# Transposing y on the sync queue instead of on TensorE: the background phases of a long convolution with a phase MLP

## The chip, the cores and the metric

The kernel runs on one core of a Trainium2 chip. That core has five engines that run side by side: TensorE (PE; its weight loads are listed as PEld), VectorE (DVE), ScalarE (ACT), GpSimd (POOL) and SyncE (SP). Transfers between HBM and the on-chip memory are issued by an engine's queue (here SP, ACT and POOL) and carried out by 16 DMA engines. The metric is the device time of one execution in microseconds, less is better. Before the change it is 1988.78 us, the median of three runs (1986.59 to 1993.94).

## The reference

```python
def _attn_ref(x, h):                       # x: 8 x 5696 x 128, h: 5696 x 128
    L = 2 * S
    Yf = np.fft.rfft(x, n=L, axis=1) * np.fft.rfft(h, n=L, axis=0)[None]
    return np.fft.irfft(Yf, n=L, axis=1)[:, :S, :]

def _moe_ref(x, w_theta, w_tok_r, w_tok_i, w_ch):
    theta = x @ w_theta
    zr, zi = x * np.cos(theta), x * np.sin(theta)
    y = einsum('ts,bsd->btd', w_tok_r, zr) + einsum('ts,bsd->btd', w_tok_i, zi)
    u = x + y
    return u + np.maximum(u @ w_ch, 0.0)
```

The output of the first function is the input of the second. Call it y, as the kernel does: 5696 tokens, 8 batches, 128 channels. The token mixing, two 5696 x 5696 matrices against 8 x 128 columns, is by far the largest part of the arithmetic.

## The kernel before

First comes the convolution, with matmuls in place of the FFTs. It leaves y in HBM as `yt_hbm`, channel by channel: for each of 128 channels and each batch a row of 5696 tokens. The token mixing follows. It runs in two passes p over the input tokens (0 to 2815, then 2816 to 5631; the last 64 tokens apart). In each pass the output tokens are taken in pairs of row blocks of 128: block tt together with block 22 + tt. A pair goes over 11 blocks of input tokens in four stretches of 3, 3, 3 and 2. Each pair forms seven products by Strassen's scheme instead of eight, in the order M3, M4, M5, M2, M1, M7, M6, and adds them into four tiles c at the pair's end (VectorE, L1399). The weights arrive through POOL's queue in a ring of six places (L669), are transposed by VectorE (`wt`, L972), summed for Strassen's products (L981), and used by TensorE (L1392).

The input of the second pass is not ready when the first pass begins. Its zr and zi are made in the background of the first pass, in "background phases": one for each of the 23 token tiles 22 to 44 and each half of the batches, 46 in all, one in every stretch of a pair but the last, so three per pair. A list `spread` holds them, each as functions:

- `load` (L995): the sync queue loads `yT`, 128 channels x 4 batches x 128 tokens. It is called two phases ahead; the pool has three buffers.
- `first` (L1000 to L1003), behind the second product of the stretch: TensorE transposes `yT` into PSUM (`tpz`, tag "misc", four transposes), ScalarE copies it to the small room (`yt_room`, 512 columns at the end of the ring's tile, one room for all), and the sync queue stores it as token rows in `y2_hbm`. The pairs later add these rows as the `x` of `x + y` (`addend`, L1085).
- `second`, behind the fifth product: `phases_b`. TensorE makes theta from `yT` (L552, PSUM tag "misc"). ScalarE rounds and copies (L554, L555), VectorE subtracts (L556), ScalarE takes the absolute value and the two sines (L572, L573, L576). VectorE multiplies both with the rows in the small room (L587, L588). The sync queue stores the results as four pieces in `z_hbm` (L611).

Tile 44 has 64 tokens only. The function `aside` takes the next entry from `spread`, runs its `first`, calls the `load` of the entry after the next, and later runs its `second`. After the phases, `spread` goes on with `bg_left` entries, and in the second pass with `u_stage` entries, which also use the small room.

What the sync queue does in a pair beside that: four loads of addends (L1085), four stores of partial sums (L1107). A queue works in its order, so an issue that waits holds up all that stands behind it. In the first pass from the third pair on, the order on each engine is the tile scheduler's; it sorts by readiness and priority, and puts in the waits between writers and readers of a tile. Each transfer of the sync queue also takes one of eight semaphores in turn.

Of the kernel before, what the change touches and what calls it, by code (L numbers as in the profile page):

```python
# [23 lines left out]
def kernel(  # L24
# [10 lines left out]
    nc = tc.nc  # L35
    B, S, D = x.shape
    assert D == 128
    P = 128
# [14 lines left out]
    y2_hbm = y2_hbm_h.ap()  # L53
# [43 lines left out]
    yt_hbm = nc.dram_tensor("yt_hbm", (D, B, S), BF16, kind="Internal").ap()  # L97
# [554 lines left out]
    def small(at, n):  # L652
        return ring["all"][:, WB + BT + at:WB + BT + at + n]
# [5 lines left out]
    def yt_room():  # L659
        return small(0, 4 * P).rearrange("p (b n) -> p b n", b=4)  # L660
# [79 lines left out]
    def load_b(p, j, pool, eng=nc.scalar):  # L740
        t_ = tile_b(p, j, pool)
        for z in range(2):
            if p == 0:
                eng.dma_start(
                    t_[:, :4096].rearrange("p (q r w) -> p q r w", q=2, r=2)[:, :, z],
                    zr_hbm[j].rearrange("q i (s r) z n -> (i s) q r (z n)", r=2)[:, :, z])
            else:
                eng.dma_start(
                    t_[:, z * 2048:(z + 1) * 2048].rearrange("p (q n) -> p q n", q=2),
                    z_hbm[z, j].rearrange("q i (s r) n -> (i s) q (r n)", r=2))  # L750
# [98 lines left out]
    for g, (bp, dh) in enumerate(groups):  # L849
        st = {}  # L850
# [85 lines left out]
    spread = []  # L936

    def open_mixing():

        nonlocal bp, cp, wlp, ybp  # L940
        xa.close()
        bp, cp, wlp, ybp = (ctx.enter_context(tc.tile_pool(name=name, bufs=bufs, reuse_waits="tile"))
                            for name, bufs in (("bpool", 1), ("cpool", 1), ("wlpool", 2), ("ybpool", 3)))
        load_b(0, NJ - 2, bp)
        sides["cs"] = [addend(0, n, t, h) for n, (t, h) in enumerate(((0, 1), (22, 0), (0, 0), (22, 1)))]
        load_b(0, NJ - 1, bp)
        spread.extend(bg_phase(t, h) for t in list(range(24, 34)) + [22, 23, 44] + list(range(34, 44)) for h in range(2))
        spread.extend(bg_left(g) for g in range(0, NT, 4))
        spread[0][0]()
        spread[1][0]()  # L950

    for j in range(NJ):
        owed += [(j, k, lambda j=j, k=k: sum_ops(bts_of[0][j])[k]()) for k in range(5)]
# [12 lines left out]
    def half(z, ti, h):  # L966

        return z[ti].rearrange("p b d -> p (b d)")[:, h * 512:h * 512 + 512]
# [20 lines left out]
    def bg_phase(t, h):  # L989
        st = {}  # L990
        m = min(P, S - t * P)

        def load():
            st["yT"] = yT = ybp.tile([P, 4, P], BF16, tag="yb", name="yT")
            nc.sync.dma_start(yT[:, :, :m], yt_hbm[:, 4 * h:4 * h + 4, t * P:t * P + m])  # L995

        def first():
            tpz = mps.tile([P, 4, P], BF16, tag="misc", name="tpz")
            for b in range(4):
                nc.tensor.transpose(tpz[:m, b, :], st["yT"][:, b, :m], ident_bf)  # L1000
            st["yb"] = yb = yt_room()
            nc.scalar.activation(yb[:m], tpz[:m], AF.Copy)  # L1002
            nc.sync.dma_start(half(y2_hbm, t, h)[:m], yb[:m].rearrange("p b d -> p (b d)"))  # L1003

        def second():
            phases_b(t, st["yb"], 4 * h, 4, st["yT"][:, :, :m], cp, mps, "misc", nc.vector,
                     tags=where_bg["tags"], m=m)
        return load, first, second

    def bg_left(g):  # L1010

        n = min(4, NT - g)
        st = {}

        def load():
            st["wl"] = wl = ybp.tile([P, 4, 2, KL], BF16, tag="yb", name="wl")
            for r, a in enumerate((moe_w_tok_r, moe_w_tok_i)):
                if g + n < NT:
                    nc.gpsimd.dma_start(
                        wl[:, :n, r, :],  # L1020
                        bass.AP(tensor=a.tensor, offset=a.offset + g * P * S + 2 * H,
                                ap=[[S, P], [P * S, n], [1, KL]]))
                else:
                    assert n == 1
                    nc.gpsimd.dma_start(
                        wl[:S_last, 0, r, :],
                        bass.AP(tensor=a.tensor, offset=a.offset + g * P * S + 2 * H,
                                ap=[[S, S_last], [1, KL]]))

        def first():  # L1030
            wl = st["wl"]
            m = P if g + n < NT else S_last
            tpw = mps.tile([P, 4, P], BF16, tag="misc", name="tpw")
            for t in range(n):
                nc.tensor.transpose(tpw[:, t, :m],
                                    wl[:m, t, :, :].rearrange("p r k -> p (r k)"),
                                    ident_bf[:m, :m])
            wls = yt_room()
            nc.scalar.activation(wls[:, :n, :m], tpw[:, :n, :m], AF.Copy)
            nc.sync.dma_start(wl_hbm[:, g:g + n, :m], wls[:, :n, :m])  # L1040
        return load, first, nothing
# [30 lines left out]
    def addend(p, k, ti, h, m=P):  # L1072

        tag = f"c{k}"
        if p == 1:
            tag = ("c0", "c1", "c2", "c3", "red", "mag")[tags["n"] % 6]
            tags["n"] += 1
        c = cp.tile([P, 512], F32, tag=tag, name=f"c{k}")
        if p == 0 and ti in (22, 23):
            yT = cp.tile([P, 4, P], BF16, tag=f"yy{k}", name=f"yy{k}")  # L1080
            nc.sync.dma_start(yT, yt_hbm[:, 4 * h:4 * h + 4, ti * P:ti * P + P])
            return c, yT
        if p == 0:
            yy = cp.tile([P, 512], BF16, tag=f"yy{k}", name=f"yy{k}")
            nc.sync.dma_start(yy[:m], half(y2_hbm, ti, h)[:m])  # L1085
            return c, yy
        nc.sync.dma_start(c[:m], half(cp_hbm, ti, h)[:m])
        return c, c
# [104 lines left out]
    nxt, second, st, ms_of = None, None, {}, {}  # L1193
    ordered = ExitStack()
    for i, (k, p, tt, j0, s0, nj) in enumerate(stretches):
# [40 lines left out]
                in_place(j)  # L1236
        if woven:
            nxt, step = nxt
        def aside(first_of, second_of):
            nonlocal second  # L1240
            if first_of and spread and (p == 1 or (tt > 1 and not end_of_pair)):
                where_bg["tags"] = ("c2", "c3") if j0 + s0 == TJ else ("red", "mag")
                _, first, second = spread.pop(0)
                first()
                if len(spread) > 1:
                    spread[1][0]()
            if second_of and second is not None:
                second()
                second = None

        if tt is None:
            if p:
                aside(True, False)
# [6 lines left out]
            for j in range(nj):  # L1260
                jj = j0 + s0 + j
                for r in range(2):
                    b = [x[:, r, :] for x in bts[jj]]
# [6 lines left out]
            if p:  # L1270
                aside(False, True)
                for f in {0: (lambda: safe(NJ - 2),), TJ: (lambda: safe(NJ - 1),),
                          2 * TJ: (lambda: in_place(NJ - 2), lambda: in_place(NJ - 1))}.get(j0 + s0, ()):
                    f()
# [64 lines left out]
        if classic:  # L1339
            for n in range(4):  # L1340
                for j in range(nj):
                    last = product(a, j0 + s0 + j, j, n, range(2))
                    if p == 0 and (n * nj + j) % 4 != 3:
                        sum_some(1)
                    if p == 0 and (n * nj + j) % 3:
                        y_some(1, last)
                if end_of_pair and n % 2:
                    (c12, z12), (c21, z21), (c11, z11), (c22, z22) = cs
                    out_of = (((c11, z11, 0), (c12, z12, 1)), ((c21, z21, 2), (c22, z22, 3)))[n // 2]
                    for h, (c, z, m_) in enumerate(out_of):  # L1350
                        if p:
                            nc.tensor.matmul(ms[m_], wl[n // 2], zl[h], start=False, stop=True)
                            nc.vector.tensor_tensor(c, z, ms[m_], op=add)
                            continue
                        if n == 1:
                            nc.tensor.matmul(ms[m_], ident_bf, z, start=False, stop=True)
                        else:
                            for b in range(4):
                                nc.tensor.matmul(ms[m_][:, b * D:(b + 1) * D], z[:, b, :], ident_bf,
                                                 start=False, stop=(b == 3))  # L1360
                        nc.scalar.activation(c, ms[m_], AF.Copy)
                aside(n == 0, n == 2)
# [92 lines left out]
```

## Time and profile before

| | |
|---|---|
| median of three runs | 1988.78 us (1986.59 to 1993.94) |
| profiled execution | 1985.37 us, span 1983.6 us, mean granted TensorE clock 0.993 |
| TensorE busy | 1922.2 us (97%) |
| VectorE busy | 1560.4 us (79%) |
| ScalarE busy | 642.7 us (32%) |
| DMA engines, mean busy share 560 to 960 us | 0.92 |
| tpz transposes (L1000) | 184, first at 464.7, last at 988.7 us |
| copies to the small room (L1002) | 46, median 597 ns |
| y stores from the small room (L1003) | issue median 535 ns, landing 1.7/4.5/6.9 us (min/median/max) |
| yT loads (L995) | landing 2.3/5.0/10.1 us |

The profile is of one execution. A group's line names the line of the kernel, the engine, the operation, what it writes and reads, how often, and then busy time and mean; idle time before an instruction stands in brackets with what ended it. On a timeline the two leading numbers are start and duration in us, several equal instructions in a row being merged. Matmuls are pipelined: their listed durations overlap, and the distance between starts is what one costs. The "share" of the DMA engines is the time that packets took, summed over queues, against the 16 engines' time; it can exceed 1.

### The profile page before, as it was taken

The numbers are of one execution on the slowest core, as the hardware profiler recorded it, in microseconds if no ns is written. First come the engines' busy times: TensorE is split into PE (matmuls) and PEld (weight loads), VectorE is DVE, ScalarE is ACT, GpSimd is POOL, SyncE is SP. The second block draws the span as 40 slices with busy tenths as digits, with TensorE's granted clock in tenths as the row PEclk, the third lists the DMA queues.
The fourth block names the chain that finished last, engine by engine and source line by source line (L and its number), as shares of the span: only waits on it lengthen the run. The fifth ranks groups of instructions, "written<-read, shape, count | busy, mean of one in ns | idle before, by whom it ended". The sixth has DMA issues, their size and how long they took to land.

```text
span 1983.6 us, 41205 instructions
## 1 busy us (share of the span) xinstructions
PE 1922.2 (97%) x15757; PEld 1060.6 (53%) x15757; DVE 1560.4 (79%) x2855; ACT 642.7 (32%) x960; POOL 976.7 (49%) x1746
## 2 busy tenths in 40 slices
PE   5899999899999999999999999999999999999998
PEld 5798997544444444444444444444444444444444
DVE  8877888876888888888877678686776877767767
ACT  6899997812233333323310001011111111111111
POOL 8636324445354544536475645445455354453540
PEclk9899999999999999999999999999999999999999
DMA  9999869998898998989999899768789688787883
GB/s 114 71 102 141 96 108 256 260 234 159 178 176 176 172 175 160 185 171 177 173 166 162 143 298 194 122 122 155 137 140 155 125 151 145 130 152 130 150 151 83
DMA packets 487829, 312.01 MB, mean 157 GB/s; under 512 B 184071, under 2 KB 448423, under 8 KB 486647
## 3 DMA queue, kind: packets, MB, share of 16 engines
q0 software_dynamic: 322160, 156.41, 62.3%
q1 hardware_dynamic: 158304, 139.22, 23.9%
q10 hardware_dynamic: 7168, 13.76, 2.0%
q8 instruction: 123, 2.02, 0.4%
q14 instruction: 74, 0.61, 0.1%
HBM read 354.37 MB, written 90.29 MB: 224 GB/s over the span
## 4 chain that ended last, share of the span: by engine, by line
PE 69%; DMA 4%; DVE 3%; POOL 1%; issue 1%; ACT 0%; ACTq 0%; DVEq 0%; SPq 0%; POOLq 0%
PE m L1392 61%; PE m L1304 3%; DMA b<-z_hbm 2%; DVE c L1399 1%; POOL ring L669 1%; PE utp L1052 1%; PE v L1059 1%; PE m L1396 1%; DVE wt L972 1%; PE m L1268 1%; DMA ring<-in_moe_w_tok_r_dram 1%; PE tpz L1000 0%; PE misc L1304 0%; PE theta_ps L552 0%; DMA ring<-in_moe_w_tok_i_dram 0%
## 5 line engine op out<-in xcount | busy, mean ns | idle before, releaser
L669 POOL DMA_DIRECT2D ring<-in_moe_w_tok_i_dram x720 | 388.0, 547 | 658.3 <-DVE wt L972 576.0
L669 POOL DMA_DIRECT2D ring<-in_moe_w_tok_r_dram x720 | 387.1, 548 | 117.8 <-DVE wt L972 68.5
L972 DVE STREAM_TRANSPOSE wt<-ring 128x384 f32<-128x384 f32 (+2 forms) x720 | 359.7, 525 | 99.9 <-PE m L1392 65.6
L1392 PE MATMUL m<-b,wt 128*128 128x512 bf16 x1640 | 388.3, 379 | 1.9 <-DVE wt L972 1.7
L1392 PEld LDWEIGHTS <-wt 128*128 128x128 bf16 x1804 | 176.1, 98 | 215.8 <-DVE wt L972 4.3
L1399 DVE TENSOR_TENSOR c<-c,m 128x512 f32<-128x512 f32 x412 | 266.7, 672 | 0.4 <-PE m L1392 0.4
L1054 ACT ACTIVATE ring<-utp 128x512 bf16<-128x512 bf16 x85 | 50.7, 597 | 575.8 <-PE utp L1052 575.8
L139 POOL DMA_DIRECT2D x<-in_x_dram x128 | 99.6, 807 | 89.8 <-PE ps L255 83.5
L432 PE MATMUL ps<-r_u,uv 128*128 128x128 f16 x1024 | 126.2, 223 | 6.6 <-DVE uv L408 3.0
L432 PEld LDWEIGHTS <-uv 128*128 128x128 f16 x2048 | 121.7, 100 | 8.8 <-issue 4.6
L432 PE MATMUL ps<-r_v,uv 128*128 128x128 f16 x1024 | 125.8, 223 | 0.0
L408 DVE TENSOR_TENSOR uv<-xs,hs 128x1024 f16<-128x1024 f16 x192 | 117.4, 662 | 5.1 <-ACT xs L404 3.6
L1304 PE MATMUL m<-b,wt 128*128 128x512 bf16 x440 | 106.8, 380 | 3.9 <-DMA b<-zr_hbm 2.3
L1049 ACT ACTIVATE ub<-c 128x512 bf16<-128x512 f32 x88 | 55.1, 628 | 161.4 <-DVE c L1399 81.9
L404 ACT ACTIVATE xs<-ps 128x1024 f16<-128x1024 f32 x96 | 88.4, 992 | 5.6 <-PE ps L278 3.1
L1304 PEld LDWEIGHTS <-wt 128*128 128x128 bf16 x528 | 50.9, 98 | 62.6 <-issue 5.0
L554 ACT ACTIVATE red<-theta_ps,magic 128x512 f32<-128x512 f32 (+1 forms) x46 | 31.6, 687 | 128.8 <-PE theta_ps L552 99.5
L1002 ACT ACTIVATE ring<-tpz 128x512 bf16<-128x512 bf16 (+1 forms) x46 | 27.4, 597 | 140.6 <-PE tpz L1000 124.0
L880 DVE TENSOR_TENSOR b<-b 128x1024 bf16<-128x1024 bf16 x100 | 61.6, 685 | 4.6 <-DMA y_hbm<-b 4.4
L278 PEld LDWEIGHTS <-w_t 64*128 64x128 f16 x3240 | 55.0, 98 | 14.2 <-issue 8.0
L1061 DVE SCALAR_TENSOR_TENSOR c<-v,c 128x512 f32<-128x512 f32 x88 | 60.1, 685 | 2.6 <-PE v L1059 2.6
L572 ACT ACTIVATE mag<-red 128x512 f32<-128x512 f32 (+1 forms) x46 | 29.0, 631 | 93.5 <-DVE red L556 93.5
(2935 smaller groups left out, 3679.9 us busy)
## 6 DMA issues: line engine op xcount, KB each, us to landing
ring<-in_moe_w_tok_r_dram POOLq DMA_DIRECT2D x352, 96.0 KB, 4.6
ring<-in_moe_w_tok_i_dram POOLq DMA_DIRECT2D x352, 96.0 KB, 4.9
ring<-in_moe_w_tok_r_dram POOLq DMA_DIRECT2D x352, 80.0 KB, 4.5
ring<-in_moe_w_tok_i_dram POOLq DMA_DIRECT2D x352, 80.0 KB, 3.9
cp_hbm<-c SPq DMA_DIRECT2D x88, 256.0 KB, 2.4
c<-cp_hbm SPq DMA_DIRECT2D x88, 256.0 KB, 4.6
out_dram<-c SPq DMA_DIRECT2D x88, 256.0 KB, 4.4
yy<-y_hbm SPq DMA_DIRECT2D x84, 128.0 KB, 2.4
```

Of the source, the lines that this page charges most:

```text
L139: nc.gpsimd.dma_start(x16[p0:p1, e, n0:n0 + 16, :HD], bass.AP(tensor=src.tensor, offset=src.offset + (p0 * N2 + n0) * D + dh * HD, ap=[[N2 ...
L404: nc.scalar.activation(xs[:, :, :, :CHK[c][1]], ps, AF.Copy)
L408: nc.vector.tensor_tensor(uv[e][:, :, :, c0:c0 + ck], xs_of[c][:, e:e + 1, :, :ck].to_broadcast([P, 2, HD, ck]), h_part(c), op=mult)
L432: nc.tensor.matmul(o, uv_t[e][:, r, d * K1:d * K1 + P], r_, start=(r == 0), stop=(r == 1))
L669: nc.gpsimd.dma_start(wb[32 * i:32 * i + 32, :ng, :nj * 64], bass.AP(tensor=a.tensor, offset=a.offset + row0 * S + p * H + i * QR + j0 * 6 ...
L880: return [lambda f=f, x=x: f(*x) for f, x in ((nc.vector.tensor_sub, (bt[M3], b12, b22)), (nc.vector.tensor_sub, (bt[M4], b21, b11)), (nc. ...
L972: nc.vector.transpose(wt.rearrange("p j t r -> p (j t r)").bitcast(F32).rearrange("p (j g t) -> p g j t", j=TJ, g=4)[:, :ng, :nj], wb[:, : ...
L1049: nc.scalar.activation(ub[:m].rearrange("p b d -> p (b d)"), c[:m], AF.Copy)
L1061: nc.vector.scalar_tensor_tensor(c[:m], v[:m], 0.0, c[:m], op0=ALU.max, op1=ALU.add)
L1304: ins = nc.tensor.matmul(ms[n // 2 * 2 + h], a[n][:, j, :, r], bts_of[p][jj][n % 2 * 2 + h][:, r, :], start=(n % 2 == 0 and jj == 0 and r ...
L1392: nc.tensor.matmul(ms[q], a[q][:, j, :, r], bts[jj][q][:, r, :], start=(jj == 0 and r == 0), stop=(jj == NJ - 1 and r == 1 and q not in left))
L1399: nc.vector.tensor_tensor(c, z, ms[q], op=op)
```

## The change

For full tiles the rows in the small room no longer come from TensorE and ScalarE. A new function `turned` takes the small room and issues four transposing transfers on the sync queue, one per batch, each of 128 channels x 128 tokens straight out of `yt_hbm`. `first` of a full tile only issues the store of the rows. `turned` is called for the next phase right after the `second` of the one before, and for the first phase when the mixing opens. `yT` is still loaded, for theta. The half tile 44, `bg_left` and `u_stage` stay as they were.

```diff
         spread[0][0]()
         spread[1][0]()
+        spread[0][3]()
...
+        def turned():
+            if m == P:
+                st["yb"] = yb = yt_room()
+                for b in range(4):
+                    nc.sync.dma_start_transpose(yb[:, b:b + 1, :], yt_hbm[:, 4 * h + b, t * P:t * P + P])
+
         def first():
+            if m == P:
+                nc.sync.dma_start(half(y2_hbm, t, h), st["yb"].rearrange("p b d -> p (b d)"))
+                return
             tpz = mps.tile([P, 4, P], BF16, tag="misc", name="tpz")
             for b in range(4):
                 nc.tensor.transpose(tpz[:m, b, :], st["yT"][:, b, :m], ident_bf)
...
-        return load, first, second
+        return load, first, second, turned
...
+        def turn_next():
+            if spread and len(spread[0]) == 4:
+                spread[0][3]()
+
         def aside(first_of, second_of):
...
-                _, first, second = spread.pop(0)
+                _, first, second = spread.pop(0)[:3]
                 first()
                 if len(spread) > 1:
                     spread[1][0]()
             if second_of and second is not None:
                 second()
                 second = None
+                turn_next()
```

## The prediction

> **What bounds the kernel now.** I read the page first (engine shares, then the costliest groups), then the stretches of the stage in which the background phases run (465 to 1000 us), then that stage's timeline.
>
> The page's first two lines, and from the view of line 1002 the copy that goes:
>
> ```profile
> span 1983.6 us, 41205 instructions
> PE 1922.2 (97%) x15757; PEld 1060.6 (53%) x15757; DVE 1560.4 (79%) x2855; ACT 642.7 (32%) x960; POOL 976.7 (49%) x1746
> L1002 ACT ACTIVATE ring<-tpz x46: 590/597/598, 465.1 to 988.9; 128x512 bf16<-128x512 bf16 x44, 64x512 bf16<-64x512 bf16 x2
> ```
>
> Two stretches of that stage (columns: busy us and instructions of PE, PEld, DVE, ACT, POOL; clock; DMA share; GB/s):
>
> ```profile
> 560.00:640.00 80.00, 80.00 (x411) 37.85 (x410) 67.48 (x132) 25.55 (x41) 38.69 (x72) 1.00 0.95 178
> 1000.00:1060.00 60.00, 59.88 (x293) 27.63 (x292) 43.61 (x88) 3.58 (x6) 40.10 (x71) 1.00 1.09 178
> ```
>
> TensorE has no gap, VectorE is busy 0.84 of the time, ScalarE a third. So a microsecond off TensorE's list is worth a microsecond, as long as VectorE keeps up. Does it? The timeline, TensorE first, then VectorE around the third phase of a pair of row blocks and around the pair's end:
>
> ```profile
> 572.67 0.39 PE L1000 MATMUL tpz<-ident_bf,yT 128*128 128x128 bf16 x4
> 572.90 0.60 PE L1392 MATMUL m<-ring,out__11532 128*128 128x512 bf16 x2
> 573.48 0.54 DVE L981 TENSOR_TENSOR out__11542<-wt 128x768 bf16<-128x768 bf16 x1
> 574.08 1.07 PEld L1392 LDWEIGHTS <-out__11542 128*128 128x128 bf16 x6 [0.22 <-DVE out__11542 L981]
> ```
>
> ```profile
> 582.99 0.69 DVE L587 TENSOR_TENSOR red<-red,ring 128x512 bf16<-128x512 f32 x1 [0.50 <-ACT red L573]
> 590.62 0.69 DVE L587 TENSOR_TENSOR red<-red,ring 128x512 bf16<-128x512 f32 x1 [0.28 <-ACT red L573]
> 593.41 0.56 DVE L981 TENSOR_TENSOR out__11697<-wt 128x768 bf16<-128x768 bf16 x1 [1.07 <-PE m L1392]
> 598.82 0.43 DVE L981 TENSOR_TENSOR out__11783<-wt 128x512 bf16<-128x512 bf16 x1 [0.35 <-PE m L1392]
> 599.28 0.58 DVE L972 STREAM_TRANSPOSE wt<-ring 128x384 f32<-128x384 f32 x1
> 599.78 0.65 DVE L587 TENSOR_TENSOR red<-red,ring 128x512 bf16<-128x512 f32 x1
> 600.95 0.68 DVE L1399 TENSOR_TENSOR c<-yy,m 128x512 f32<-128x512 bf16 x1
> ```
>
> A pair takes 34.58 us (the first phase's theta matmuls stand at 576.78, the next pair's at that distance): 7 products x 11 blocks x 2 = 154 matmuls of 512 columns and six groups of four small ones (three phases, each four transposes and four theta matmuls), 160 places of 0.216 us. The phases' first multiplications L587, the only VectorE reader of the small room, stand at 582.99, 590.62, 599.78, then 617.57: gaps of 7.63, 9.16 and 17.79 us, the same in nearly every pair. Between the first two and the third VectorE has idle time (1.07, 0.79, 1.00 and 0.35 us, mostly waiting for TensorE to give a weight buffer back), some 3.2 us that can swallow a delay. From 598.82 on it has none until the next pair's first phase: third multiplication, twelve additions, the sums. And at 574.08 the weights arrive just as TensorE wants them (0.1 us before their matmul). So **a delay of the third multiplication goes straight to TensorE**.
>
> The sync queue behind the first phase, and the landing times of that stage:
>
> ```profile
> 583.71 1.09 SPq L611 DMA_DIRECT2D z_hbm<-red  x2
> 584.89 1.20 SPq L611 DMA_DIRECT2D z_hbm<-mag  x2
> 586.18 0.55 SPq L1003 DMA_DIRECT2D y_hbm<-ring  x1
> ```
>
> ```profile
> yy<-y_hbm SPq DMA_DIRECT2D x48, 128.0 KB, 2.3
> yT<-yt_hbm SPq DMA_DIRECT2D x33, 128.0 KB, 4.8
> z_hbm<-red SPq DMA_DIRECT2D x64, 64.0 KB, 4.3
> z_hbm<-mag SPq DMA_DIRECT2D x64, 64.0 KB, 4.6
> y_hbm<-ring SPq DMA_DIRECT2D x32, 128.0 KB, 4.5
> ```
>
> **The change, part by part.**
>
> *TensorE loses 44 groups of four transposes* (two partial phases keep theirs). Each group takes 0.23 us on the timeline (572.67 to 572.90), one place of 0.216: 44 x 0.216 = 9.5 us. Of that, the first phase's group lies in VectorE's full run, where TensorE has only 0.1 us in hand, so a third of it would come back as a wait: the gain is 6.3 to 9.5 us, 0.43 to 0.65 per pair. The page TensorE: Matmul & The Clock Gate of the Trainium skill (Part 4, PE-mode transpose) gives about 275 ns for one transpose in a kernel's context. By it 176 of them would be worth 48 us, and the hidden case below would be 1937; the rows say 9.5, since the four overlap.
>
> *ScalarE loses 44 copies of 0.597 us* (26 us). It idles two thirds of the stage: nothing. *PSUM* "misc" is free earlier, so one theta matmul of every third phase stands 12 matmuls earlier in the built order, and one VectorE subtraction three places earlier; its partners stay, so nothing.
>
> *The sync queue gains 176 issues.* At 0.55 to 0.6 us each that is 12 x 0.6 = 7 us per pair beside the 14 it has now, of 34.6: not full. Partial sums that go out (L1107) move some 2 us back, still about 6 us ahead of the next use of their buffers. The 16 engines gain 176 x 128 = 22,528 packets of 256 B; this queue's packets take 0.308 x 16 x 400 us / 47,538 = 41 ns, so 58 us per engine over 535, a share of 1.03 where 0.92 was. At 1.09 (1000 to 1060 us) TensorE still had 59.88 of 60 us: hidden. The four turned ahead at the start stand at 412 us, long before use.
>
> *The order of the small room is where the price lies.* There is one room. The next phase's transposes are issued behind this phase's four z stores; they also overwrite what this phase's y store (now L1006 of the changed text) reads, and that store itself waits for its own transposes. Until it has landed the sync queue stands, with addends, y loads and partial sums behind it. In the built order each first transpose does wait for that store. Per pair, with m1, m2, m3 the three multiplications:
> - z stores end 3.15 us after m1 (582.99 to 586.14); the four transposes are issued and the last lands after G. m2 is at m1 + 3.15 + G + 0.1 or later.
> - Then the second phase's y store goes out and lands 4.5 us later (its row); its z stores are through before that if G is large.
> - Then the third phase's transposes, again G, and m3.
>
> So m3 - m1 is at least 3.15 + G + 4.5 + G + 0.1 = 7.75 + 2G, against 16.79 now. From m3 to the next m1 VectorE needs its 17.79 us, full, and there the transposes have time. Per pair the change is the larger of -0.43 and 2G - 9.04. It turns at **G = 4.5 us**.
>
> No row shows a transposing transfer, so G is bounded. Below: four loads issued in a row (yy, 1.99 us for four) with a landing of 2.3: 1.5 + 2.3 = 3.8. Above: the longest z issue, 1.22 us, and the usual landing: 3 x 1.22 + 4.4 = 8.1. I take the four z stores, on this queue, right ahead of the transposes, amid the weight loads: 3 x 0.6 + 4.4 = 6.2. A y load of the same 512 rows of 256 B says about the same (4.8 as one transfer, and three more issues). Then 2 x 6.2 - 9.04 = 3.4 us a pair. The 46 phases make 15 triples and one over; one triple holds the partial tile, whose transposes stay on TensorE. 14 x 3.4 = 47 us. TensorE's saving vanishes inside VectorE's wait.
>
> **Sum:** the profiled execution took 1985.4 us (span 1983.6), 3.4 below the median of 1988.8. 1985.4 + 47 = 2032 us; from the median 2036.
>
> **Rivals.**
> 1. *The transposes are hidden.* G below 4.5: the room is full in time and TensorE's places are gained, 1985.4 - 6.3 to - 9.5 = 1976 to 1979 us. For it: 32 KB a piece, and yy loads of 128 KB land in 2.3 us. Against it: those land in the pause of the weight loads; here the z stores and weights are in the queues. This is the other side, and G = 4.5 decides.
> 2. *Each transpose is dearer than a plain transfer*, in issue or because 16 engines must meet: G = 8.1, 7.2 us a pair, 100 us, 2086. No row speaks against it. The page VectorE: DVE Perf Modes of the Trainium skill (The three transpose paths) has 1309 ns for a 128x128 transpose by DMA against 390 on TensorE, and prefers TensorE. As a pitch that is an estimate of 3 x 1.31 + 4.4 = 8.3 and 2091; as the whole of it, 5.2 for four, 2005. No trace here shows which.
> 3. *Weights come late*, the engines being fuller. They are issued when VectorE frees a ring place and VectorE waited for them 4.7 us in all from 500 to 990; 11% on landings of 4.7 is 0.5 us, under the 3.2 in hand. It would add 0.5 x 15 = 8 us at worst to the case that holds, and has no chance of its own.
>
> **How the numbers follow.** Forecast (G from 4.8 to 7.3, +10 to +78 us) 0.46; hidden 0.27, with the few cases of a small loss; dearer 0.27. One measurement tells about 0.5%, 10 us, from no change. The hidden case gains 6 to 9.5, mostly inside that: faster 0.08, same 0.19, slower 0.73. Range 1977 to 2090: it leaves out the upper part of rival 2 and a gain above all the TensorE places. The forecast's own range is 1995 to 2063.
>
> **What would show it.** Right: the third multiplication waits for a DMA into the room, m3 - m1 near 20 us, pairs of 38 us, TensorE waiting for VectorE some 3 us at each pair's end, DMA issues of y stores just behind landings. The transposes' own rows give G. Wrong: gaps still 7.6 and 9.2 and pairs of 34.0 (hidden); issues far over 0.6 us (dearer); VectorE waiting for weights (rival 3); or a y store that lands in 2 us, which moves the turning point up by 1.2.

## The result, and the profile after

The changed kernel takes 2096.06 us (median of five runs, 2091.90 to 2101.14), the one before 1990.90 in the same five rounds: a ratio of 1.0541 (95% interval 1.0521 to 1.0561), 105 us slower. The forecast was 2032 us. Its direction and its place were right; its size was not, and the time lies 6 us above the upper end of its range.

The profiled execution took 2096.06 us, with a span of 2094.3 us (110.7 more than before). All of it lies where the background phases run. From the first of their multiplications L587 to the last it takes 629.5 us (480.1 to 1109.6), where it took 517.9 (481.0 to 998.8): 111.6 us more. From the last one to the end it is 984.7 us, and 984.8 before.

The page's first two lines, after (the engines' busy time, share of the span, instructions):

```profile
span 2094.3 us, 40798 instructions
PE 1937.0 (92%) x15408; PEld 1055.8 (50%) x15581; DVE 1554.9 (74%) x2855; ACT 616.0 (29%) x916; POOL 978.3 (47%) x1746
```

TensorE and VectorE have about as much work as before, and a smaller share of a longer span. They wait. On what, the view of line 1002 tells, the transposing transfers (issue ns min/median/max; then who waited for them, us and times; then the time to landing):

```profile
L1002 SPq DMA_TRANSPOSE ring<-yt_hbm x176: 1110/1232/2596, 414.2 to 1098.8; - x176
...
  DVE red L587: 152.2, 28
DMA to landing us min/median/max: 2.3/5.1/9.2
```

28 waits: the second and the third phase of 14 pairs, 5.4 us each on average. One issue holds the queue for 1.232 us. I had taken 0.6.

The sync queue through one pair of row blocks (start, duration of the issues; equal ones merged):

```profile
649.92 1.10 SPq L611 DMA_DIRECT2D z_hbm<-red  x2
651.12 1.19 SPq L611 DMA_DIRECT2D z_hbm<-mag  x2
652.36 5.55 SPq L1002 DMA_TRANSPOSE ring<-yt_hbm  x4
...
661.58 0.34 SPq L1006 DMA_DIRECT2D y_hbm<-ring  x1
...
664.76 5.48 SPq L1002 DMA_TRANSPOSE ring<-yt_hbm  x4
674.12 0.35 SPq L1006 DMA_DIRECT2D y_hbm<-ring  x1
```

VectorE's first multiplications in the same pair, with the idle time before each and what ended it:

```profile
649.20 0.69 DVE L587 TENSOR_TENSOR red<-red,ring 128x512 bf16<-128x512 f32 x1 [0.50 <-ACT red L573]
661.62 0.69 DVE L587 TENSOR_TENSOR red<-red,ring 128x512 bf16<-128x512 f32 x1 [5.24 <-DMA ring<-yt_hbm]
674.25 0.69 DVE L587 TENSOR_TENSOR red<-red,ring 128x512 bf16<-128x512 f32 x1 [6.74 <-DMA ring<-yt_hbm]
692.07 0.69 DVE L587 TENSOR_TENSOR red<-red,ring 128x512 bf16<-128x512 f32 x1 [0.50 <-ACT red L573]
```

Read the two together. The z stores follow the first multiplication, and the transposes start 3.16 us after it (649.20 to 652.36). The y store of the second phase, which waits for them, goes out at 661.58: G, from the first transposing issue to the last landing, is 9.2 us, and 9.4 in the next phase. Taken in this way over all 28 waits, G is 9.0 us on average (6.3 to 10.8). In the pair shown the last of the four issues starts 4.3 us behind the first and lands 4.8 us later; over the 28 waits it starts 4.1 us behind on average. The gaps between the multiplications are 12.42, 12.63 and 17.82 us (10.7 to 14.6, 12.1 to 13.1 and 15.8 to 18.2 in the other 13 pairs that wait), where they were 7.63, 9.16 and 17.79. The third gap is VectorE's full run and hasn't moved.

TensorE at the third phase, and two stretches of the stage (busy us and instructions of PE, PEld, DVE, ACT, POOL; granted clock; DMA share; GB/s):

```profile
669.72 1.03 PE L1407 MATMUL m<-b,out__12136 128*128 128x512 bf16 x4
676.53 1.89 PE L1407 MATMUL m<-b,out__12138 128*128 128x512 bf16 x4 [5.78 <-DVE out__12138 L982]
```

```profile
560.00:640.00 80.00, 68.31 (x310) 30.52 (x314) 53.68 (x106) 18.60 (x30) 34.08 (x64) 0.91 0.94 150
675.00:679.00 4.00, 2.47 (x6) 0.89 (x7) 4.00 (x8) 0.00 (x0) 0.00 (x0) 0.50 0.51 131
```

TensorE waits 5.78 us for a sum that stands behind the third multiplication on VectorE. DMA engines are no busier than before (0.94 of these 80 us, and 0.95 in the same 80 before).

And the landing times from 560 to 1060 us:

```profile
z_hbm<-red SPq DMA_DIRECT2D x68, 64.0 KB, 2.2
y_hbm<-ring SPq DMA_DIRECT2D x33, 128.0 KB, 2.0
```

The y store lands in 2.0 us (4.5 before). It goes out when the transposes have landed and the weight loads are held up: from 661 to 667 us the DMA share is 0.69. The prediction had named this as a sign that its turning point was wrong.

### The profile page after: what moved, and what is told of

It reads as the page before. It is cut to its first block, busy times and chain, and to the rows that moved or that the text cites. A ratio compares the mean times of both kernels' runs of the same rounds, so it can differ in the third digit from the quotient of the medians.

```text
span 2094.3 us, 40798 instructions
## 1 busy us (share of the span) xinstructions
PE 1937.0 (92%) x15408; PEld 1055.8 (50%) x15581; DVE 1554.9 (74%) x2855; ACT 616.0 (29%) x916; POOL 978.3 (47%) x1746
## 2 busy tenths in 40 slices
DMA packets 515990, 317.80 MB, mean 152 GB/s; under 512 B 212231, under 2 KB 476583, under 8 KB 514807
## 3 DMA queue, kind: packets, MB, share of 16 engines
q1 hardware_dynamic: 186464, 145.01, 25.2%
## 5 line engine op out<-in xcount | busy, mean ns | idle before, releaser
L1407 PEld LDWEIGHTS <-wt 128*128 128x128 bf16 x1804 | 181.2, 101 | 237.8 <-issue 34.9
L587 DVE TENSOR_TENSOR red<-red,ring 128x512 bf16<-128x512 f32 (+1 forms) x46 | 31.8, 692 | 162.1 <-DMA ring<-yt_hbm 152.2
L554 ACT ACTIVATE red<-theta_ps,magic 128x512 f32<-128x512 f32 (+1 forms) x46 | 31.6, 687 | 387.8 <-PE theta_ps L552 341.3
L1319 PEld LDWEIGHTS <-wt 128*128 128x128 bf16 x528 | 50.9, 98 | 63.0 <-issue 5.1
L278 PEld LDWEIGHTS <-w_t 64*128 64x128 f16 x3240 | 55.1, 98 | 13.1 <-issue 7.1
L1407 PE MATMUL m<-ring,wt 128*128 128x512 bf16 x160 | 56.0, 434 | 5.8 <-DVE c L1414 4.7
```

The lines of the kernel that those rows point to most:

```text
L278: nc.tensor.matmul(ps[:, e, j * HD:(j + 1) * HD], w_t2[rows, slot(e, c0 + j), N2 * (1 - ri):N2 * (3 - ri)], a_st["a"][rows, ri * K1 + c0 + ...
L1319: ins = nc.tensor.matmul(ms[n // 2 * 2 + h], a[n][:, j, :, r], bts_of[p][jj][n % 2 * 2 + h][:, r, :], start=(n % 2 == 0 and jj == 0 and r ...
L1407: nc.tensor.matmul(ms[q], a[q][:, j, :, r], bts[jj][q][:, r, :], start=(jj == 0 and r == 0), stop=(jj == NJ - 1 and r == 1 and q not in left))
```

## The experiments

Theory W, from the prediction: one small room makes a chain of transposes, store and transposes, and its cost is G, twice a pair. Q: the price is the transposing transfer's issue on the sync queue (rival 2 in one form). C: the price is contention, the transposing packets on the DMA engines. Ratios are to the kernel before, run beside each on the same chip.

| run | what is done | ratio (95% interval) | us |
|---|---|---|---|
| first_only | only the first phase of three turned by transfers | 0.9978 (0.9962 to 0.9993) | 1988.27 |
| plain | four plain loads in their place | 1.0211 (1.0190 to 1.0232) | 2035.36 |
| wide | one transposing transfer of 128 x 512 | 1.0235 (1.0211 to 1.0259) | 2039.80 |
| not_second | second phase by TensorE | 1.0280 (1.0257 to 1.0302) | 2047.64 |
| not_third | third phase by TensorE | 1.0184 (1.0158 to 1.0210) | 2030.55 |
| z_on_act | z stores on ScalarE's queue | 1.0480 (1.0455 to 1.0505) | 2088.56 |
| rooms | two small rooms | 1.0334 (1.0313 to 1.0355) | 2061.19 |
| rooms_late_store | two rooms, y store later | 1.0098 (1.0068 to 1.0129) | 2012.28 |
| rooms_1_and_3 | the same, second phase by TensorE | 1.0007 (0.9992 to 1.0022) | 1988.29 |
| rooms_wide | the same as rooms_late_store, one wide transfer | 0.9994 (0.9973 to 1.0016) | 1983.48 |
| rooms_plain | the same, four plain loads | 0.9983 (0.9969 to 0.9998) | 1983.29 |

### Only the first phase

```diff
-            if m == P:
+            if full:          # full = m == P and q % 3 in (0,), q the phase's number
```

> The changed kernel, but only the first of a pair's three background phases (15 full ones) is turned by transfers; the second and third go by TensorE and ScalarE as before. The first phase has 17.8 us since the third of the pair before, more than the 12.4 us that z stores and transposes take. Theory W: no wait, 0 to 3 us under the kernel before. Theories C and Q: a third of the loss, +35 us.

Measured: 0.9978. The room of a first phase is filled between one pair's third phase and the next pair's first, where 17.8 us lie. VectorE's multiplications in one pair:

```profile
623.88 0.69 DVE L587 TENSOR_TENSOR red<-red,ring 128x512 bf16<-128x512 f32 x1 [0.50 <-ACT red L573]
631.88 0.69 DVE L587 TENSOR_TENSOR red<-red,ring 128x512 bf16<-128x512 f32 x1 [0.51 <-ACT red L573]
640.51 0.65 DVE L587 TENSOR_TENSOR red<-red,ring 128x512 bf16<-128x512 f32 x1
658.30 0.69 DVE L587 TENSOR_TENSOR red<-red,ring 128x512 bf16<-128x512 f32 x1 [0.51 <-ACT red L573]
```

No wait for a transfer into the room is left, and a pair takes 34.42 us (34.58 before). So a transposing transfer costs nothing by being there, where it has time. This speaks for W and against a cost that comes with every transfer. It is the only kernel with the reference's own computation that is faster than the one before, by 0.2%, and that barely: the interval ends at 0.9993, and of the 4 us only 2.4 stand in the stage itself (515.5 us from the first multiplication to the last, 517.9 before).

### What G is made of: plain loads, and one wide transfer

```diff
-                    nc.sync.dma_start_transpose(yb[:, b:b + 1, :], yt_hbm[:, 4 * h + b, t * P:t * P + P])
+                    nc.sync.dma_start(yb[:, b, :], yt_hbm[:, 4 * h + b, t * P:t * P + P])
```

> The changed kernel with four plain loads of 32 KB into the room in place of the four transposing ones, same source rows, same place in the queue. The token rows are then not turned: y rows of 44 phases and what is made of them are other numbers than the reference's; the work is the same. Theory W with my prices of plain transfers: issue 0.55 us, last landing 6.2 us after the first issue, multiplications 9.4 us apart, pairs 1.9 us longer: +27 us; with landings of 2 to 3 us instead of 4.4 it is hidden and 6 to 10 us are gained. Theory C (crossbar): no loss. Theory Q: 0.55 of 1.3 us an issue, +45 us.

```diff
-                for b in range(4):
-                    nc.sync.dma_start_transpose(yb[:, b:b + 1, :], yt_hbm[:, 4 * h + b, t * P:t * P + P])
+                t0 = min(t, 40) * P
+                nc.sync.dma_start_transpose(yb, yt_hbm[:, 4 * h, t0:t0 + 4 * P])
```

> The changed kernel with one transposing transfer of 128 x 512 in place of four of 128 x 128. It reads 512 neighbouring tokens of one batch, so the rows of y of 44 phases are other numbers than the reference's; bytes and blocks are the same, rows read are 1 KB instead of 256 B. If the issue is priced per instruction (1.3 us once), the room is full some 5 us after the issue, multiplications 8.2 us apart: hidden, 6 us under the kernel before. If it is priced per block of 16 x 128, the issue takes about 5 us, the last landing stays near 9 us: +90 to +105 us (W). Theory C: between, as the engines move the same bytes in fewer packets.

Measured: 1.0211 and 1.0235, 42 and 47 us where the change costs 105. The sync queue, first of plain, then of wide:

```profile
647.23 2.06 SPq L1002 DMA_DIRECT2D ring<-yt_hbm  x4
...
654.04 0.32 SPq L1006 DMA_DIRECT2D y_hbm<-ring  x1
```

```profile
648.94 1.21 SPq L1002 DMA_TRANSPOSE ring<-yt_hbm  x1
654.88 0.35 SPq L1006 DMA_DIRECT2D y_hbm<-ring  x1
```

Four plain issues take 2.06 us, four transposing ones 5.55. G is 6.8 us with plain loads here (6.6 on average over the 27 waits, 5.7 to 7.9). So my 6.2 was about the price of plain loads. They cost 42 us, near the 47 forecast for the change, but that is luck in part: G is larger than 6.2, and the y store, which I had counted, costs nothing (see below). Of what I expected of this run it is no hit either: W gave 27 us, for it had G at 6.2 and the y store free, and Q gave 45. The one wide transfer moves the same bytes through the same path, and G is 5.9 (6.5 on average over its 26 waits, 4.9 to 8.0). Its issue takes 1.228 us at the median, as long as that of a transfer a quarter its size. So between these two sizes an issue's price is by instruction and not by block of 128 x 128, and three issues fewer per phase are worth 58 of the 105 us (105 less 47). My expectation of wide was too sharp: neither hidden nor 90 to 105. Even with one issue, landing takes 6.0 us at the median, and G stays above the turning point.

### One of the two waits taken away

```diff
+        full = m == P and q % 3 in (0, 2)     # not_second; (0, 1) in not_third
```

> One room; the first and third phase are turned by transfers, the second by TensorE and ScalarE. Only the third multiplication is late: 12.5 us after the second instead of 9.2. Theory W: no time in hand there, 3.3 us a pair, +43 to +47 us, more than twice the run with the second late although the delay is shorter. Theory C: two thirds of the loss, +70 us, the same as the run with the second late.

> One room; the first and second phase of a pair are turned by transfers, the third by TensorE and ScalarE. Only the second multiplication is late: 12.2 us after the first instead of 7.6. Theory W with my reading that VectorE has 3.2 us in hand there: 4.6 - 3.2 = 1.4 us a pair, +14 to +20 us. If a late second multiplication costs in full: +55 to +64 us. Theory C: two thirds of the loss, +70 us.

Measured: not_second 1.0280, 55 us, not_third 1.0184, 37 us, of 105 for both. The 70 us of C came in neither. W had the order right (the late third multiplication costs more) and both sizes too low: 43 to 47 and 14 to 20. VectorE's multiplications in not_second:

```profile
640.50 0.69 DVE L587 TENSOR_TENSOR red<-red,ring 128x512 bf16<-128x512 f32 x1 [0.51 <-ACT red L573]
648.22 0.69 DVE L587 TENSOR_TENSOR red<-red,ring 128x512 bf16<-128x512 f32 x1 [0.50 <-ACT red L573]
660.21 0.69 DVE L587 TENSOR_TENSOR red<-red,ring 128x512 bf16<-128x512 f32 x1 [3.22 <-DMA ring<-yt_hbm]
678.04 0.69 DVE L587 TENSOR_TENSOR red<-red,ring 128x512 bf16<-128x512 f32 x1 [0.50 <-ACT red L573]
```

The second multiplication is on time again (7.72 us), the third 11.99 us behind it and not 9.16. In three pairs on end the first and the third stand 22.8, 20.3 and 19.7 us apart, 16.79 before: a mean of 4.1 us more a pair, x 14 = 58. In three pairs of not_third the second comes 12.5, 12.7 and 11.5 us after the first, and the third 20.7, 19.2 and 20.5. So of 4.8, 5.1 and 3.9 us of delay 0.9, 2.7 and 0.2 are caught up by VectorE, less than the 3.2 that I had counted; no pair catches up more than 2.7. But this run isn't clean, for it has a wait of its own (waits from 480 to 1110 us: us, times, longest):

```profile
ACT ring L1013 <- DMA y_hbm<-ring: 63.4, 9, 8.0
PE theta_ps L552 <- ACT ring L1013: 37.9, 14, 7.4
```

ScalarE's copy of the third phase must wait until the second's y store has left the room, and the theta matmuls stand behind that copy for their PSUM place. What VectorE can swallow by itself shows in another run, rooms below. Its second multiplications come late without such a wait behind them, and in six of its pairs the third follows after 6.0 us, 3.2 less than 9.16, with 0.2 us of idle time left between them. So the 3.2 us are there, where nothing else is in the way.

### The z stores off the queue

```diff
-                    nc.sync.dma_start(z_hbm[r, j, q_, i], z[rows])
+                    nc.scalar.dma_start(z_hbm[r, j, q_, i], z[rows])
```

> The changed kernel (one room) with the four z stores of a phase issued on ScalarE's queue, so that the next phase's transposes stand right behind the multiplication's end on the sync queue: 2.4 us less between two multiplications, 10.0 instead of 12.4. Theory W: pairs of 17.8 + 20.0 = 37.8 us instead of 42.6, a loss of 14 x 3.2 = +45 us. Theory Q (issue time on the sync queue as such): little better than the changed kernel, +85 us. ScalarE gains 4 x 0.6 us of issues a phase, of which it has three quarters idle.

Measured: 1.0480, 96 us. That is more than either theory expected, W's by far. The sync queue in one pair:

```profile
651.25 5.93 SPq L1002 DMA_TRANSPOSE ring<-yt_hbm  x4
660.86 0.32 SPq L1006 DMA_DIRECT2D y_hbm<-ring  x1
...
663.30 5.03 SPq L1002 DMA_TRANSPOSE ring<-yt_hbm  x4
```

With nothing ahead of them the transposes still start 2.44 us after the y store (3.18 in the change, 661.58 to 664.76): they overwrite what it reads and wait until it has landed. Store and z issues had stood side by side, and only the longer of the two counts. So here taking the z stores away gains 0.7 us (3.18 less 2.44) and not the whole 3.2. Behind a pair's first multiplication it gains more: the transposes start 1.3 us after it, 3.3 in the change (means over all waits). Together that is 2.5 us a pair, but G has grown from 9.0 to 9.6, which takes half of it back. Why G grew wasn't tested.

### Two rooms

```diff
-    def yt_room():
-        return small(0, 4 * P).rearrange("p (b n) -> p b n", b=4)
+    def yt_room(n=0):
+        return small(4 * P * n, 4 * P).rearrange("p (b n) -> p b n", b=4)
...
-                st["yb"] = yb = yt_room()
+                tags["room"] = 1 - tags["room"]
+                st["yb"] = yb = yt_room(tags["room"])
...
                 first()
+                turn_next()
...
                 second()
                 second = None
-                turn_next()
```

The ring's tile grows by 128 columns for it, and some small constants share one tile to make place. Lines move by one: the multiplication is L586.

> The changed kernel with a second small room behind the first (the ring's tile grows by 256 B a partition, a few constants are packed together to pay for it); a phase's four transposes go into the other room, so that they may be issued one phase earlier. All 176 transposes stay, on the same queue. Theory W (the loss is the wait for the room: VectorE's multiplication stands until transposes that could only be issued after the phase before have landed): the wait is gone, gaps between the first multiplications are back at 7.6 and 9.2 us, and TensorE's saved places are gained: 6 to 10 us under the kernel before. Theory C (transposing transfers slow the 16 DMA engines and with them the weights, wherever they stand): about +105 us, as in the changed kernel. Theory Q (the sync queue is held up by 1.3 us an issue, and what stands behind it is late): +60 to +105 us.

Measured: 1.0334, 67 us. VectorE hardly waits for the room any more (5.3 us in all, 152.2 in the change); W said that this would be all. The sync queue, ScalarE and VectorE around a pair's end:

```profile
636.70 5.07 SPq L1002 DMA_TRANSPOSE ring<-yt_hbm  x4
641.86 1.95 SPq L1096 DMA_DIRECT2D yy<-y_hbm  x4
644.48 0.32 SPq L1006 DMA_DIRECT2D y_hbm<-ring  x1
644.85 3.36 SPq L1118 DMA_DIRECT2D cp_hbm<-c  x4
```

```profile
654.41 0.69 ACT L553 ACTIVATE red<-theta_ps,biases 128x512 f32<-128x512 f32 x1 [8.63 <-DMA cp_hbm<-c]
```

```profile
656.13 0.69 DVE L555 SCALAR_TENSOR_TENSOR red<-red,mag 128x512 f32<-128x512 f32 x1 [4.88 <-ACT mag L554]
```

The stores of partial sums now stand behind four transposing issues, and behind a y store that waits for their landing. They go out later, and land in 7.4 us (500 to 1000 us; 2.2 before); that they then meet the weight loads is how I read it. The second phase of a pair works in the places of two of the tiles c, so ScalarE can't round its theta before those stores have landed, and VectorE waits for ScalarE. From 480 to 1110 us VectorE's waits for ScalarE's copy of theta (L554) add up to 64.0 us (12.2 before), those for weights to 34.3 (4.7), and those for z stores that still read a tile which VectorE wants to write to 26.3 (1.5). The first and the last hang on stores of the sync queue: for the larger part the wait for the room has turned into one for the queue.

```diff
-                nc.sync.dma_start(half(y2_hbm, t, h), st["yb"].rearrange("p b d -> p (b d)"))
+                ins = nc.sync.dma_start(half(y2_hbm, t, h), st["yb"].rearrange("p b d -> p (b d)"))
+                tc.add_manual_dep(ins.ins, where_bg["behind"].ins.name, ...)   # behind the last matmul of the second product
```

> The two rooms again, with the store of the y rows tied behind the second product of its own stretch, so that the sync queue no longer reaches it before its transposes have landed. In the two-room run VectorE no longer waited for the room; it waited for ScalarE, and ScalarE for the stores of partial sums that stood on the sync queue behind a y store which waited for its transposes, and behind four transposes of 1.3 us. Theory W+Q (the price is waits on the queue, which this order takes away): VectorE's gaps 7.6 and 9.2, partial sums stored in time, 5 to 10 us under the kernel before. Theory C (transposes take the engines from the weights): still +50 us or more.

Measured: 1.0098, 20 us. With two rooms and a y store that no longer waits long at the head of the queue, 85 of the 105 us are gone; the gain of 5 to 10 us that I expected isn't reached. These waits are left (480 to 1110 us; the second line is VectorE waiting for weights):

```profile
ACT red L553 <- DMA cp_hbm<-c: 51.9, 8, 11.9
DVE wt L972 <- DMA ring<-in_moe_w_tok_r_dram: 32.1, 13, 4.8
```

### What the last 20 us are

Three runs, all on top of rooms_late_store: its second phase given back to TensorE, one wide transfer, and four plain loads, with the edits shown above.

> Two rooms and the late y store, but the second phase of a pair goes by TensorE and ScalarE (29 phases turned by transfers). In the built order no transposes then stand between a pair's last z stores and its partial sums on the sync queue. If what is left of the loss with two rooms (about +20 us) is the late partial sums behind four issues of 1.3 us (theory Q): gone, 3 to 6 us under the kernel before. If it is weights that come late because transposes share the engines (theory C): two thirds of it stay, +10 to +14 us.

> Two rooms and the late y store, with one transposing transfer of 128 x 512 a phase in place of four of 128 x 128 (it reads 512 neighbouring tokens of one batch, so y rows of 44 phases are other numbers than the reference's). The queue has 1.2 us of issue a phase instead of 5.5; the crossbar moves the same blocks. Theory Q: 6 to 10 us under the kernel before. Theory C by the crossbar: still +15 to +20 us.

> Two rooms and the late y store, with four plain loads of 32 KB a phase, not transposing (y rows of 44 phases are not turned, other numbers than the reference's). 2.1 us of issue a phase, the same packets of 256 B. Theory Q: 4 to 9 us under the kernel before. Theory C by packets on the engines: still +15 to +20 us; by the crossbar: no loss.

Measured: 1.0007, 0.9994 and 0.9983. All three lose the 20 us. None reaches the gain that Q expected (3 to 10 us): the medians lie between 2 us above and 3 us below that of the kernel before. VectorE's multiplications in rooms_wide, and 80 us of its stage, with the same 80 of rooms_plain behind it:

```profile
619.61 0.69 DVE L586 TENSOR_TENSOR red<-red,ring 128x512 bf16<-128x512 f32 x1 [0.51 <-ACT red L572]
626.54 0.65 DVE L586 TENSOR_TENSOR red<-red,ring 128x512 bf16<-128x512 f32 x1
635.80 0.65 DVE L586 TENSOR_TENSOR red<-red,ring 128x512 bf16<-128x512 f32 x1
653.58 0.69 DVE L586 TENSOR_TENSOR red<-red,ring 128x512 bf16<-128x512 f32 x1 [0.50 <-ACT red L572]
```

```profile
560.00:640.00 80.00, 79.58 (x384) 36.98 (x391) 67.47 (x133) 21.98 (x35) 41.84 (x79) 1.00 1.17 192
```

```profile
560.00:640.00 80.00, 79.63 (x385) 36.99 (x391) 68.15 (x134) 21.97 (x35) 40.51 (x76) 1.00 1.04 192
```

Both kernels put the rows of all 44 full phases through transfers. In rooms_wide the DMA share is 1.17 and TensorE has next to no gap (0.4 of 80 us), with a transposing transfer in every full phase. In rooms_late_store the share is lower (1.07 from 500 to 1000 us, 1.11 in rooms_wide) and the loss is there. The packets hardly differ (515,990 in the whole of rooms_late_store, 511,765 in rooms_wide, 487,829 before). So more packets and fuller engines (C) don't by themselves make the loss. What differs is three issues per phase.

That it is the queue's time also shows within rooms_late_store, for its pairs aren't alike. Five late ones take 33.96 to 33.98 us, as in rooms_wide, and four of these have all twelve transposes of 128 x 128. The stores of partial sums ahead of a pair of 38.9 us (its first multiplication stands at 597.0) and ahead of one of 33.98 (846.8):

```profile
595.02 0.86 SPq L1120 DMA_DIRECT2D cp_hbm<-c  x2
597.32 2.00 SPq L1120 DMA_DIRECT2D cp_hbm<-c  x2
...
840.65 0.86 SPq L1120 DMA_DIRECT2D cp_hbm<-c  x2
842.12 1.24 SPq L1120 DMA_DIRECT2D cp_hbm<-c  x2
```

The last of the first four lands 8.9 us after the multiplication, that of the other four 1.0 us after it. In the five pairs where it is 7.8 us or more, a pair takes 36.0 to 38.9 us; in the six where it is 4.7 us or less, 33.98 to 34.5 (left out is the pair behind the half tile, 35.3 us here and 35.5 before). In rooms_wide it lands about 4 us ahead of the multiplication. The queue's issues take 28 to 30 us of such a fast pair, 16 to 17 of a pair in rooms_wide and 12 to 13 before, so a queue that is behind has little time to catch up. It caught up in the pair that holds the half tile, with four transposing issues instead of twelve, and the other fast pairs follow that one. This compares pairs of one execution and is no experiment. Weights do come late in this run, too (5.4 to 5.7 us to landing for the larger ones, 4.9 to 5.2 in rooms_wide; VectorE waits 32.1 us for them, and 5.5 to 6.5 in the three runs above). But the pair from 846.8 us has 2.6 us of such waits and loses nothing. Whether late weights add to the loss of the slow pairs wasn't told apart.

Here is also what the change can bring when all is hidden: pairs of 33.97 us for 34.58, 0.61 less. From the first multiplication to the last it is 5.3 us (512.6 for 517.9), a quarter of a percent of the whole. The medians of the runs on one chip differ by 2.8 us, and their interval (0.9973 to 1.0016) includes no change.

## Why the prediction failed in size

*What bounds the kernel, and where the price lies*: right. The room's order was the price, m3 - m1 is what it lengthens, and a late third multiplication goes straight to TensorE. Two rooms or a phase with time to spare take it away.

*TensorE's 0.43 to 0.65 us a pair*: right. It shows only where the transfers are hidden, 0.61 in rooms_wide. The first phase's share doesn't all come back as a wait: with that phase alone changed a pair is 0.16 us shorter. Over 15 triples 0.61 would be 9 us; from the first to the last multiplication it is 512.6 us for 517.9, 5.3 less. The rest goes in the stage's first two pairs, which are longer and not shorter: 34.9 and 34.7 us, 33.2 and 34.3 before. Why they are wasn't looked into.

*ScalarE, PSUM*: right, nothing to be seen of them.

*The sync queue gains 176 issues at 0.55 to 0.6 us*: here the prediction failed. The row it took was that of the z stores, and a transposing issue takes 1.232 us at the median. In the pair shown the 12 of them take 15.7 us and not 7. All the queue's issues of that pair come to 28.4 us, where a pair before had 12.6 (the prediction said 14). In a pair of 34.6 us that leaves 6 to wait in; the prediction's figures leave 14. It fits this that two rooms alone weren't enough. The packets were mis-counted as well: the queue has 28,160 more (186,464 for 158,304), not 22,528.

*G = 6.2*: the mis-sized term. The prediction let the last of the four transposes start 1.8 us behind the first (3 x 0.6) and land 4.4 us later. It starts 4.1 us behind (mean of the 28 waits), which is 2.3 us more, and lands 4.9 us later. So G was 9.0. The upper bound of 8.1 was too low too: the longest z issue, 1.22 us, is about what a transposing issue takes at the median, so it was no bound, and the landing had none but the usual 4.4. In the sum, with 9.0 for 6.2, two G a pair and 14 triples, this is 78 us more. (A slip beside it: by the prediction's rule G = 4.8 gives 8 us, not 10.)

*The y store lands 4.5 us later*: wrong in the other direction. It landed in 2.0 us at the median (1.7 to 3.3 between the second phase and the third), inside the 3.2 us that the z stores hold the queue in all but one of the twelve pairs whose landing the trace has, and so it cost next to nothing of its own. The rule becomes m3 - m1 = 2 x (3.15 + G + 0.1) = 6.5 + 2G, not 7.75 + 2G, 1.25 us a pair or 17.5 in all. The sum of the prediction with both terms mended is 47 + 78 - 17.5 = 108 us, and 110.7 were measured between the profiled executions. z_on_act shows that the y store is only covered, not gone: without the z stores in front, the queue waits for it instead. The G at which the change would cost nothing moves from 4.5 to 5.1 (16.79 = 6.5 + 2G).

*From m3 to the next m1 17.79 us*: 17.82, right. *DMA engines at 1.03 are hidden*: right as far as rooms_wide shows it, with a share of 1.11 from 500 to 1000 us and no loss.

*The rivals.* "Hidden" needed G below its turning point, and with one room none of the three fillings came below it on average (9.0, 6.6 and 6.5 us); two single waits of wide were at 4.9, never both of a pair. With two rooms and few issues it does occur, at 0.61 us a pair. "Each transpose is dearer" was what happened: 100 us forecast for it, 105 measured. That it is so close is luck, since its G of 8.1 was too small and its y store cost too much. It was given 0.27 against the forecast's 0.46, though no row spoke against it. The page VectorE: DVE Perf Modes of the Trainium skill (The three transpose paths), with 1309 ns for a 128x128 transpose by DMA, was nearer than my rows: read as the distance between the starts of two transposes, it stands against 1.35 here (4.06 over 3, mean of the 28 waits). As a time to landing it would not fit (5.1). "Weights late": VectorE waited 13.9 us for weights from 480 to 1110 us, 4.7 before; it lies under the waits for the room.

## What to carry to other kernels

A transfer that takes over work from an idle-looking engine must be costed by its issue time on the queue first, and an operation that the trace doesn't show needs an upper bound that is more than the longest of another operation's rows. Where a buffer exists once, write out the loop fill, use, store, fill again and see how often it lies inside the bottleneck's period: here it fitted between pairs, at no cost, and not within a pair, where VectorE waited 5.4 us a time. A wait that is removed at the buffer comes back at the next thing that the same queue does, so look at what stands behind the new issues, too.

## What the hardware showed that I had not expected

The time of a transposing issue was the same for both sizes tried: 1.232 us for 128 x 128 and 1.228 for 128 x 512 of bf16 (medians of the changed kernel and of wide), against 0.439 for a plain load of 32 KB on the same queue.

The granted clock of TensorE fell at the waits of several microseconds. At the gap of 5.78 us shown above, which ends at 676.53, it was 0.50 from 675 to 679 us and 1.00 again from 682; around a wait of 0.99 us before it (661 to 667 us) it was 1.00. Over the stage from 520 to 1110 us it was 0.92, where before it was 1.00 (500 to 1000). No cost of it shows here: VectorE is full in that stretch, and its 17.82 us are those of before. The page TensorE: Matmul & The Clock Gate of the Trainium skill describes this, in HAM oscillation — how this bites in real kernels: waits for data that outlast the activity monitor's window put the array back to half rate. The 0.50 agrees.

The same transfer landed after very different times in these kernels, though its size was the same. The stores of partial sums landed in 2.2 us before, 7.4 in rooms and 2.6 in rooms_wide; the y stores in 4.5 before and 2.0 after.
